# Two cached decode attentions on one core: A's keys and values by fours of heads, ahead of B's pairs

## The chip, the core and the metric

The kernel runs on one core of a Trainium2 chip. The metric is device time in microseconds, as the median of the runs; the kernel before took 249.97 us (three runs, 249.94 to 250.91). A profile is one further execution, taken with the hardware profiler.

## What is computed

Two independent attention blocks, A and B, decode one token each. Each has 32 query heads, 16 key/value heads of 128 elements and a cache of 8,192 keys; A uses only the last 2,048 of its keys, B uses all. Everything is bf16, and the two results are joined.

```python
    def _A_ref(x, k_cache, v_cache, wq, wo):
        B, Sq, D = x.shape
        Hq, Dh = 32, 128
        Hkv, Sk = k_cache.shape[1], k_cache.shape[2]
        W = min(4096, max(256, Sk // 4))
        rep = Hq // Hkv
        q = (lambda x, *d: x.transpose(*d))((x @ wq).reshape(B, Sq, Hq, Dh), 0, 2, 1, 3)
        k = jnp.repeat(k_cache[:, :, Sk - W:, :], rep, axis=1)
        v = jnp.repeat(v_cache[:, :, Sk - W:, :], rep, axis=1)
        scores = jnp.einsum("bhqd,bhkd->bhqk", q, k) * (Dh ** -0.5)
        p = _softmax(scores, axis=-1)
        o = jnp.einsum("bhqk,bhkd->bhqd", p, v)
        return (lambda x, *d: x.transpose(*d))(o, 0, 2, 1, 3).reshape(B, Sq, Hq * Dh) @ wo
...
    return jnp.concatenate([a, b], axis=-1)
```

B's function is the same without the slices of k and v.

The inputs that are read are A's K and V (16.8 MB), B's K and V (67.1 MB), two wq and two wo (18.9 MB together): 102.8 MB.

## The kernel before

The program is a list of operations per engine, in a hand-written order. `Prog.op` adds one to an engine with the names of those it depends on, `Prog.load` a DMA, and `emit` turns names into semaphore waits (L78). Each engine works its list strictly in order. All large loads are issued by SP (L208, L211, L219) into one SBUF ring of 144 KB a partition; `place` hands out the ring in order, and a load that overlaps an older one waits for that one's last reader. Because SP is in order too, a load that waits holds back the loads behind it.

The loads, in order: wq of A and of B (each 4 MB and a 0.5 MB tail), then for each of the eight pairs of key/value heads K of B (4 MB), K of A (1 MB), V of B, V of A; then wo of A in one piece and wo of B in six. A pair of B lies with 32 KB rows, head h on partitions 64h to 64h + 63. A pair of A has two rows of 4 KB on each partition, one for each head.

First the queries: x is brought onto the partitions (L263 to L280: `xd`, `xT`, `xr`), then `qmm` (L295) multiplies by wq in 16 groups of five matmuls, `qe` evicts, `qT` transposes on DVE, and `z0`, `z1` (L312, L318) copy the queries into `za` and `zb`, zero tiles that POOL has filled before (L236, L237). With the query columns at the right place of a zero tile, the scores of all slabs of a pair add up in one PSUM bank of 128x512: row 2s + r is slab s, query r.

Then for each pair p, in the order in which each engine has it:

- ten slabs of 2,048 elements, eight of B and two of A: DVE transposes K (`T`, L335) into one of three buffers `ktb`, and PE makes four matmuls of 128x512 (`S`, L345) from it;
- the maximum: `max` on DVE (L354), `mT` on PE (L356) to bring it into one row, `mrB`, `mrA`, `mxB`, `mxA` on DVE (L361 to L372) per head, `bc` on PE (L376) back to the partitions, `nb` on DVE (L378);
- `exp` on ACT (L380), with the row sums;
- `PT`: DVE transposes the weights, in two halves (L384);
- `V`: for each slab of B four matmuls of 128x512 in four column groups (L393), for each of A eight of 128x256 (L400);
- `xo0` on ACT (L407) and `xo1` on DVE (L409) evict, and `OB`, `OA` (L414, L421) fold the four groups with f32 matmuls into one column per head.

So on DVE the transposes of pair p + 1 stand behind `PT` and `xo1` of pair p, and on PE its scores stand behind `V`, `OB` and `OA` of pair p. At the end come `lsel`, `L`, `rl`, `on`, `oq`, `pm`, `oP` (the sums, the division and a regrouping, L430 to L446), the 128 output matmuls `F` (L457), a copy and the store.

Of the kernel before, what the change touches and what calls it, by code (L numbers as in the profile page):

```python
# [21 lines left out]
NB = 2 * SK // 128 * DH // SLAB  # L22
NI = NB + 2
W0 = 2 * (NB - 1)
ZW = 128 + W0
RING = 72 * 1024
# [80 lines left out]
def bass_concat_heads__sliding_block_cached__gqa_block_cached__decode_kernel(nc, A_x, A_k_cache, A_v_cache, A_wq, A_wo,  # L107
# [5 lines left out]

    ring = nc.alloc_sbuf_tensor("ring", [128, RING], BF16)
# [12 lines left out]
    za = nc.alloc_sbuf_tensor("za", [128, NP, 2, 4, 128], BF16)  # L127
    mx = nc.alloc_sbuf_tensor("mx", [128, 2], F32)
    mr = nc.alloc_sbuf_tensor("mr", [128, 8], F32)
    mexp = nc.alloc_sbuf_tensor("mexp", [128, 128], F32)  # L130
    nb = nc.alloc_sbuf_tensor("nb", [128, 2], F32)
# [4 lines left out]
    cls = nc.alloc_sbuf_tensor("cls", [128, 8], F32)  # L136
    selb = nc.alloc_sbuf_tensor("selb", [128, 16], F32)
    sela = nc.alloc_sbuf_tensor("sela", [128, 4], F32)
    par = nc.alloc_sbuf_tensor("par", [128, 2], F32)
    lsel = nc.alloc_sbuf_tensor("lsel", [128, NP, 8], F32)  # L140
    rl = nc.alloc_sbuf_tensor("rl", [128, NP * 8], F32)
# [60 lines left out]
    kv_at = {}  # L202
    for p in range(NP):
        for kind, c in (("K", ks), ("V", vs)):
            use = "T%d.%d" if kind == "K" else "V%d.%d"
            src = c[1][0, 2 * p:2 * p + 2, :, :].rearrange("h (q t) d -> (h q) (t d)", q=64)
            kv_at[kind, p, 0] = place(NB * SLAB, [use % (p, NB - 1)],
                                      lambda e, t, src=src: e.dma_start(t, src), "%sB%d" % (kind, p))  # L208
            src = c[0][0, 2 * p:2 * p + 2, SK - W_A:SK, :].rearrange("h (q t) d -> q h (t d)", q=128)
            kv_at[kind, p, 1] = place(2 * SLAB, [use % (p, NI - 1)],  # L210
                                      lambda e, t, src=src: e.dma_start(t.rearrange("q (h n) -> q h n", h=2), src),  # L211
                                      "%sA%d" % (kind, p))
# [10 lines left out]
    def slab(kind, p, s):  # L223
        t = kv_at[kind, p, s // NB]
        s %= NB
        return t[:, s * SLAB:(s + 1) * SLAB]
# [9 lines left out]
    op("pool", lambda e: e.memset(zb[:], 0.0), name="zb0")  # L236
    op("pool", lambda e: e.memset(za[:], 0.0), name="za0")  # L237
    op("pool", lambda e: e.memset(mexp[:], 0.0), name="mexp0")
    op("pool", lambda e: e.memset(onesf[:], 1.0), name="ones")
    op("pool", lambda e: e.memset(pts[:], 0.0), name="pts0")  # L240
# [3 lines left out]
    for b in range(2):  # L244
        op("dve", lambda e, b=b: e.memset(vb[b][:, :], 0.0), name="vb0.%d" % b)
# [3 lines left out]
    for h in range(2):  # L249
        op("dve", lambda e, h=h: e.tensor_reduce(  # L250
            cls[:, 2 * h:2 * h + 2], view(identf, 128, 64 * h, [[1, 2], [32, 2], [2, NB]]), AX.XY, ALU.add),
            deps=["identf"], name="clsB%d" % h)
    op("dve", lambda e: e.tensor_reduce(cls[:, 4:8], view(identf, 128, 2 * NB, [[1, 4], [32, 4]]), AX.X, ALU.add),
       deps=["identf"], name="clsA")
    op("dve", lambda e: e.tensor_reduce(selb[:], view(identf, 128, 0, [[1, 16], [32, 4]]), AX.X, ALU.add),
       deps=["identf"], name="selb")
    op("dve", lambda e: e.tensor_reduce(sela[:], view(identf, 128, 0, [[4, 2], [1, 2], [32, 4], [2, 2]]), AX.XY, ALU.add),
       deps=["identf"], name="sela")
# [3 lines left out]
    for P in range(2):  # L262
# [14 lines left out]
        for c in range(2):  # L277
            op("dve", lambda e, P=P, c=c: e.tensor_scalar(  # L278
                xrep[:, P, 4 + c, :], banks[2 * P + 1][:, 0:128], par[:, c:c + 1], None, ALU.mult),
                deps=["xT%d.4" % P, "par%d" % c], name="xr%d.%d" % (P, 1 + c))  # L280
    XR = ["xr%d.%d" % (P, c) for P in range(2) for c in range(3)]

    KT = NKT * SLAB
    for P in range(2):
        for n in range(8):
# [17 lines left out]
            else:  # L303
# [4 lines left out]
                deps=["qe%d" % u] + (["z0.%d" % i for i in range(8)] if P else []), name="qT%d" % u)  # L308
        srcs = [[512, NP], [64, 2], [1, 2], [128, 2]]
        for b in range(4):  # L310
# [5 lines left out]
            else:  # L316
                for h in range(2):
                    op("dve", lambda e, b=b, h=h: e.tensor_copy(  # L318
                        view(za, NP * 1024, h * 512 + 32 * b + 2 * (NB + h),
                             [[1024, NP], [256, 2], [128, 2], [1, 2]], 32, 32 * b),  # L320
                        view(ktb, KT, h * 256, srcs, 32, 32 * b)),
                        deps=["qT%d" % u for u in range(8)] + ["za0"], name="z0.%d" % (2 * b + h))
    Z = ["z0.%d" % i for i in range(8)] + ["z1.%d" % i for i in range(4)]


    def unit(kind, p, s):
        return "%s%s%d" % (kind, "BA"[s // NB], p)

    for p in range(NP):
        for s in range(NI):  # L330
            k = p * NI + s
            kt = ktb[:, (k % NKT) * SLAB:(k % NKT + 1) * SLAB]
            deps = [unit("K", p, s)]
            deps += ["S%d" % (k - NKT)] if k >= NKT else Z
            op("dve", lambda e, p=p, s=s, kt=kt: e.transpose(kt.bitcast(I32), slab("K", p, s).bitcast(I32)),  # L335
               deps=deps, name="T%d.%d" % (p, s))

# [12 lines left out]
            if s == 0:  # L350
                deps += ["exp%d" % (p - 2), "max%d" % (p - 2)] if p >= 2 else Z + ["qe%d" % u for u in range(16)]
# [153 lines left out]
```

## Time and profile before

Times in us. An execution has a span, from its first instruction to its last, and some time around it; the profiled one took 250.0 for a span of 248.2.

| what | value |
|---|---|
| median of the runs | 249.97 |
| the profiled execution; its span | 250.0; 248.2 |
| mean granted clock of PE | 0.82 |
| busy: PE, DVE, ACT, POOL | 181.7, 153.1, 18.1, 13.4 |
| DMA: packets, MB, GB/s over the span | 8,262, 102.92, 415 |
| packets under 8 KB | 5,564 |
| the chain that ended last: DMA, DVE, PE | 32%, 31%, 30% |
| K transposes L335 | 80 of 1.213, 92.4 |
| scores L345, from B and from A | 256 matmuls, 73.6; 64, 16.7 |
| V matmuls L393 (B) and L400 (A) | 256, 28.2; 128, 7.8 |
| folds L414 and L421 | 64 records each, 10.8 and 9.9 |
| output matmuls L457 | 128, 10.9 |

An engine's busy time says how much work it has, the chain says which work the end waited for, and the line of a group ends with the idle time ahead of it and what released it. PE's clock is granted at full or half rate, so the same matmul has two lengths: five of L295 take 2.14 us at 18.10 us, when PE has just begun, and 1.08 from 22.4 us on. Where a group's mean lies between, it mixes the two.

### The profile page before, as it was taken

Reading aid. Unit: us, or ns where it says so; the run is one execution under the profiler, and the core shown is the slowest. Engines: PE = TensorE matmul, PEld = TensorE weight load, DVE = VectorE, ACT = ScalarE, POOL = GpSimd, SP = SyncE. Lnnn points to the kernel's source line nnn. Section 1 sums busy time; section 2 is a strip of 40 time slices with the busy share of each in tenths; the row PEclk is TensorE's granted clock in tenths of the full one; section 3 lists DMA queues with packets and bytes.
Section 4 is the critical chain, followed back from the end, with each engine's and each line's share of the span. In section 5 each row is a group of like instructions: output and inputs, shape, how many; then the busy total and the mean of one; then the engine's idle time right before and its main releaser. Section 6 shows DMA issues by size and latency. Waiting matters only on the chain.

```text
span 248.2 us, 2581 instructions
## 1 busy us (share of the span) xinstructions
PE 181.7 (73%) x1085; PEld 80.7 (33%) x1085; DVE 153.1 (62%) x228; ACT 18.1 (7%) x36; POOL 13.4 (5%) x15
## 2 busy tenths in 40 slices
PE   0039994957995799379746984998489757975795
PEld 0013441313631342143224321732153124322552
DVE  8963779952885298439734873487349725972300
ACT  2001220010001000100010001000100010001000
POOL 8920000000000000000000000000000000000000
PEclk9999999795589599877987597569677957895769
DMA  7999999999999999999999999999999999999992
GB/s 264 418 490 433 422 422 416 417 428 418 427 414 434 419 458 419 436 432 431 421 429 414 434 422 428 420 422 419 433 420 433 428 433 422 436 403 457 395 406 111
DMA packets 8262, 102.92 MB, mean 415 GB/s; under 512 B 694, under 2 KB 956, under 8 KB 5564
## 3 DMA queue, kind: packets, MB, share of 16 engines
q1 hardware_dynamic: 8248, 102.77, 97.9%
q8 instruction: 8, 0.13, 0.2%
q14 instruction: 2, 0.02, 0.0%
q10 hardware_dynamic: 4, 0.00, 0.0%
HBM read 102.76 MB, written 0.00 MB: 414 GB/s over the span
## 4 chain that ended last, share of the span: by engine, by line
DMA 32%; DVE 31%; PE 30%; issue 3%; ACT 2%; SPq 0%; POOL 0%; POOLq 0%; DVEq 0%
DMA ring<-in_B_k_cache_dram 22%; DVE ktb L335 18%; DMA ring<-in_B_wo_dram 10%; PE sb L345 10%; PE vb L393 7%; DVE xdup L263 5%; PE sb L295 4%; PE qb L295 3%; DVE pts L384 3%; ACT psb L380 2%; PE ob L414 1%; DVE mx L354 1%; PE ob L421 1%; PE vb L400 1%; PE mb L356 1%
## 5 line engine op out<-in xcount | busy, mean ns | idle before, releaser
L335 DVE STREAM_TRANSPOSE ktb<-ring 128x1024 int32<-128x1024 int32 x80 | 92.4, 1213 | 11.3 <-DMA ring<-in_B_k_cache_dram 7.6
L345 PE MATMUL sb<-ktb,zb 128*128 128x512 bf16 x256 | 73.6, 443 | 11.0 <-DVE ktb L335 9.8
L345 PEld LDWEIGHTS sb<-ktb,zb 128*128 128x128 bf16 x256 | 25.6, 110 | 56.3 <-DVE ktb L335 24.2
L393 PE MATMUL vb<-ring,pts 128*16 128x512 bf16 x256 | 28.2, 619 | 21.1 <-DVE pts L384 21.1
L409 DVE COPY xo<-vb 128x512 f32<-128x512 f32 x8 | 5.5, 692 | 35.8 <-PE vb L400 35.8
L393 PEld LDWEIGHTS vb<-ring,pts 128*16 128x16 bf16 x256 | 8.5, 123 | 34.3 <-issue 34.2
L345 PE MATMUL sb<-ktb,za 128*128 128x512 bf16 x64 | 16.7, 381 | 1.3
L380 ACT ACTIVATE psb<-sb,nb 128x512 bf16<-128x512 f32 x8 | 5.5, 687 | 140.9 <-DVE nb L378 140.9
L384 DVE STREAM_TRANSPOSE pts<-psb 64x512 bf16<-64x512 bf16 x16 | 11.3, 706 | 7.0 <-ACT psb L380 6.8
L295 PE MATMUL sb<-ring,xrep 128*128 128x512 bf16 x40 | 11.2, 438 | 1.3 <-DVE xrep L278 1.3
L263 DVE COPY xdup<-xrow 1x128 bf16<-1x128 bf16 x2 | 11.3, 5660 | 0.0
L457 PE MATMUL qb<-ring,oP 128*1 128x288 bf16 x128 | 10.9, 346 | 0.5 <-DVE oP L446 0.4
L414 PEld LDWEIGHTS ob<-selb,xo 128*128 128x128 f32 x64 | 10.1, 242 | 3.4 <-ACT xo L407 3.4
L354 DVE TENSOR_REDUCE mx<-sb 128x1 f32<-128x512 f32 x8 | 5.5, 692 | 9.1 <-PE sb L345 9.1
L414 PE MATMUL ob<-selb,xo 128*128 128x4 f32 x64 | 10.8, 293 | 0.3 <-ACT xo L407 0.3
L272 PE MATMUL sb<-onesb,xrow 1*128 1x128 bf16 x4 | 0.6, 295 | 14.0 <-DVE xdup L263 14.0
L306 DVE STREAM_TRANSPOSE ktb<-qsb 128x256 int32<-128x256 int32 x16 | 7.0, 443 | 6.1 <-ACT qsb L301 5.8
L421 PE MATMUL ob<-sela,xo 128*128 128x2 f32 x64 | 9.9, 276 | 0.0
L421 PEld LDWEIGHTS ob<-sela,xo 128*128 128x128 f32 x64 | 9.5, 227 | 0.0
L295 PE MATMUL qb<-ring,xrep 128*128 128x512 bf16 x40 | 9.3, 379 | 0.0
L345 PEld LDWEIGHTS sb<-ktb,za 128*128 128x128 bf16 x64 | 4.9, 96 | 13.1 <-DVE ktb L335 9.2
L457 PEld LDWEIGHTS qb<-ring,oP 128*1 128x1 bf16 x128 | 6.1, 99 | 5.3 <-DMA ring<-in_B_wo_dram 1.2
(66 smaller groups left out, 83.0 us busy)
## 6 DMA issues: line engine op xcount, KB each, us to landing
ring<-in_B_k_cache_dram SPq DMA_DIRECT2D x8, 4096.0 KB, 27.0
ring<-in_B_v_cache_dram SPq DMA_DIRECT2D x8, 4096.0 KB, 26.8
ring<-in_A_k_cache_dram SPq DMA_DIRECT2D x8, 1024.0 KB, 28.9
ring<-in_A_v_cache_dram SPq DMA_DIRECT2D x8, 1024.0 KB, 27.2
ring<-in_A_wo_dram SPq DMA_DIRECT2D x1, 4608.0 KB, 28.2
ring<-in_A_wq_dram SPq DMA_DIRECT2D x1, 4096.0 KB, 12.2
ring<-in_B_wq_dram SPq DMA_DIRECT2D x1, 4096.0 KB, 22.3
ring<-in_B_wo_dram SPq DMA_DIRECT2D x1, 2304.0 KB, 33.4
```

The costliest lines, as they stand in the source:

```text
L263: op("dve", lambda e, P=P: e.tensor_copy(view(xdup, 256, 128 * P, [[2, 64], [1, 2]], parts=1), view(xrow, 2 * DM, P * DM + 512, [[1, 64], ...
L295: ins = e.matmul(bank[:, :], lhsT=lhsT, rhs=o, start=(k == 0), stop=(k == 4))
L306: op("dve", lambda e, n=n: e.transpose(ktb[:, n * 512:(n + 1) * 512].bitcast(I32), qsb[:, n % 2, :].bitcast(I32)), deps=["qe%d" % u] + ([" ...
L335: op("dve", lambda e, p=p, s=s, kt=kt: e.transpose(kt.bitcast(I32), slab("K", p, s).bitcast(I32)), deps=deps, name="T%d.%d" % (p, s))
L345: ins = e.matmul(sb[p % 2][:, :], lhsT=lhsT, rhs=view(ktb, KT, (k % NKT) * SLAB + 64 * c + v, [[128, 16], [2, 32]]), start=(s == 0 and c = ...
L354: op("dve", lambda e, p=p: e.tensor_reduce(mx[:, 0:1], sb[p % 2][:, :], AX.X, ALU.max), deps=["S%d" % (p * NI + NI - 1)] + (["mT%d" % (p - ...
L380: op("act", lambda e, p=p: e.activation(psb[:, :], sb[p % 2][:, :], ACT.Exp, bias=nb[:, p % 2:p % 2 + 1], scale=SCALE, accum_out=rsall[:, ...
L384: op("dve", lambda e, h=h: e.transpose(view(pts, 1024, 2 * h, [[4, 16], [64, 16], [1, 2]], 64, 64 * h), psb[64 * h:64 * h + 64, :]), deps= ...
L393: ins = e.matmul(vb[0][32 * j:32 * j + 16, :], lhsT=view(pts, 1024, 64 * s + 16 * j, [[1, 16]]), rhs=src[:, 512 * j:512 * j + 512], start= ...
L414: ins = e.matmul(ob[:, 8 * p:8 * p + 4], lhsT=xo[:, 0, 128 * t:128 * t + 128], rhs=selb[:, 4 * t:4 * t + 4], start=(t == 0), stop=(t == 3))
L421: ins = e.matmul(ob[:, 8 * p + 4 + 2 * h:8 * p + 6 + 2 * h], lhsT=xo[:, 1, 256 * h + 128 * t:256 * h + 128 * t + 128], rhs=sela[:, 2 * t:2 ...
L457: ins = e.matmul(fb[r:r + 1, 0:288], lhsT=oP[:, 1 - P, k0 + k:k0 + k + 1], rhs=wo_at[P, c][:, k * DM + 288 * n:k * DM + 288 * n + 288], st ...
```

## The change

- A's K and V are loaded before B's, in four units of four heads: row 4g + h of a load holds the 64 keys that start at 64g of head h, 16 KB, so that 8 loads of 2 MB take the place of 16 of 1 MB.
- Each unit has its own scores (four slabs in a bank of `qb`), maximum, exp, transpose `PA`, V matmuls, eviction `xoA` on ACT and fold `OA`. A partition holds one head, so a row of scores also has columns for keys of heads that are not its own; a matmul `mask` with -1e30 there starts the bank, and exp makes them 0.
- B's pairs have eight slabs in place of ten, and lose everything of A. `xo1` is gone from DVE; `xo` stays on ACT.
- The fills of `za`, `zb` and `pts` move from POOL to DVE, behind the preparation of x, and so do the small reductions for selectors; one of the two PSUM fills is gone. `za` shrinks from 8,192 to 2,432 elements a partition.
- The output columns lie by A and B, so that the product before `F` is plain.

The diff, cut:

```diff
 SLAB = 2048
-NB = 2 * SK // 128 * DH // SLAB
-NI = NB + 2
+ROW = 2 * SK // 128 * DH
+NB = ROW // SLAB
+NQ = G // 4
+TA = 4 * W_A // 128
+NA = TA * DH // SLAB
 W0 = 2 * (NB - 1)
 ZW = 128 + W0
+ZA = 128 + 24
+BIG = 1e30
 RING = 72 * 1024
 NSEM = 24
 NKT = 3
...
+    for u in range(NQ):
+        for kind, c in (("K", ks[0]), ("V", vs[0])):
+            src = bass.AP(tensor=c.tensor, offset=c.offset + (4 * u * SK + SK - W_A) * DH,
+                          ap=[[TA * DH, 32], [SK * DH, 4], [1, TA * DH]])
+            kv_at[kind, "A", u] = place(TA * DH, [("TA%d.%d" if kind == "K" else "VA%d.%d") % (u, NA - 1)],
+                                        lambda e, t, src=src: e.dma_start(t, src), "%sA%d" % (kind, u))
     for p in range(NP):
-        for kind, c in (("K", ks), ("V", vs)):
-            use = "T%d.%d" if kind == "K" else "V%d.%d"
-            src = c[1][0, 2 * p:2 * p + 2, :, :].rearrange("h (q t) d -> (h q) (t d)", q=64)
-            kv_at[kind, p, 0] = place(NB * SLAB, [use % (p, NB - 1)],
+        for kind, c in (("K", ks[1]), ("V", vs[1])):
+            src = c[0, 2 * p:2 * p + 2, :, :].rearrange("h (q t) d -> (h q) (t d)", q=64)
+            kv_at[kind, "B", p] = place(ROW, [("T%d.%d" if kind == "K" else "V%d.%d") % (p, NB - 1)],
                                       lambda e, t, src=src: e.dma_start(t, src), "%sB%d" % (kind, p))
-            src = c[0][0, 2 * p:2 * p + 2, SK - W_A:SK, :].rearrange("h (q t) d -> q h (t d)", q=128)
-            kv_at[kind, p, 1] = place(2 * SLAB, [use % (p, NI - 1)],
-                                      lambda e, t, src=src: e.dma_start(t.rearrange("q (h n) -> q h n", h=2), src),
-                                      "%sA%d" % (kind, p))
...
-    op("pool", lambda e: e.memset(zb[:], 0.0), name="zb0")
-    op("pool", lambda e: e.memset(za[:], 0.0), name="za0")
     op("pool", lambda e: e.memset(mexp[:], 0.0), name="mexp0")
     op("pool", lambda e: e.memset(onesf[:], 1.0), name="ones")
-    op("pool", lambda e: e.memset(pts[:], 0.0), name="pts0")
...
+
+    op("dve", lambda e: e.memset(za[:], 0.0), name="za0")
+    op("dve", lambda e: e.memset(zb[:], 0.0), name="zb0")
+    op("dve", lambda e: e.memset(pts[:], 0.0), name="pts0")
+    op("dve", lambda e: e.memset(vb[0][:, :], 0.0), name="vb0.0")
...
+    op("dve", lambda e: e.tensor_copy(mkr[:], view(ident, 128, 0, [[0, 128], [1, 4]], 4)),
+       deps=["ident"], name="mkr")
+    op("dve", lambda e: e.tensor_scalar(mkl[:], view(ident, 128, 0, [[0, 16], [1, 4], [0, 2]], 4), -1.0, BIG,
+                                        ALU.add, ALU.mult), deps=["ident"], name="mkl")
...
+                op("dve", lambda e, b=b: e.tensor_copy(
+                    view(za, NQ * 4 * ZA, ZA - 128 + 32 * b, [[4 * ZA, NQ], [2 * ZA, 2], [ZA, 2], [1, 8]], 32, 32 * b),
+                    view(ktb, KT, 0, [[1024, NQ], [64, 2], [1, 2], [128, 8]], 32, 32 * b)),
+                    deps=["qT%d" % u for u in range(8)] + ["za0"], name="z0.%d" % b)
+    Z = ["%s.%d" % (z, b) for z in ("z0", "z1") for b in range(4)]
+    QE = ["qe%d" % u for u in range(16)]
...
+    def scores(k, kind, src, name, lhsT, bank, start, stop, deps):
+        kt = ktb[:, (k % NKT) * SLAB:(k % NKT + 1) * SLAB]
+        op("dve", lambda e: e.transpose(kt.bitcast(I32), src.bitcast(I32)),
+           deps=[kind] + (["S%d" % (k - NKT)] if k >= NKT else Z), name=name)
+
+        def mm(e):
+            for c in range(2):
+                for v in range(2):
+                    ins = e.matmul(bank[:, :], lhsT=lhsT(2 * c + v),
+                                   rhs=view(ktb, KT, (k % NKT) * SLAB + 64 * c + v, [[128, 16], [2, 32]]),
+                                   start=(start and c == 0 and v == 0), stop=(stop and c == 1 and v == 1))
+            return ins
+        op("pe", mm, deps=[name] + deps, name="S%d" % k)
...
+    for u in range(NQ):
+        bank = qb[u % 2]
+        op("pe", lambda e, bank=bank: e.matmul(bank[:, :], lhsT=mkl[:].rearrange("p a h r -> p (a h r)"),
+                                               rhs=mkr[:].rearrange("p q h -> p (q h)"), start=True, stop=False),
+           deps=["expA%d" % (u - 2), "maxA%d" % (u - 2)] if u >= 2 else ["mkl", "mkr"] + QE, name="mask%d" % u)
+        for s in range(NA):
+            scores(u * NA + s, "KA%d" % u, slab("K", "A", u, s), "TA%d.%d" % (u, s),
+                   lambda ce, u=u, s=s: za[:, u, ce, ZA - 128 - 8 * s:ZA - 8 * s], bank, False, s == NA - 1, [])
+        op("dve", lambda e, bank=bank: e.tensor_reduce(mx[:, 4:5], bank[:, :], AX.X, ALU.max),
+           deps=["S%d" % (u * NA + NA - 1)] + (["mTA%d" % (u - 1)] if u else []), name="maxA%d" % u)
+        op("pe", lambda e: e.matmul(mb[0:1, 0:128], lhsT=mx[:, 4:5], rhs=identf[:, :], start=True, stop=True),
+           deps=["maxA%d" % u, "identf"] + (["mrA%d" % (u - 1), "nbA%d" % (u - 1)] if u else []), name="mTA%d" % u)
+        op("dve", lambda e: e.tensor_reduce(mr[0:1, 8:16], view(mb, 512, 0, [[1, 8], [8, 16]], parts=1), AX.X, ALU.max),
+           deps=["mTA%d" % u] + (["mxA%d" % (u - 1)] if u else []), name="mrA%d" % u)
+        op("dve", lambda e: e.tensor_scalar(
+            mexpa[:].rearrange("p (a m) -> p a m", m=8), view(mr, 32, 8, [[0, 16], [1, 8]], parts=1), -SCALE, None,
+            ALU.mult), deps=["mrA%d" % u] + (["bcA%d" % (u - 1)] if u else []), name="mxA%d" % u)
+        op("pe", lambda e: e.matmul(mb[:, 128:129], lhsT=mexpa[0:1, :], rhs=onesf[0:1, 0:1], start=True, stop=True),
+           deps=["mxA%d" % u, "ones"], name="bcA%d" % u)
+        op("dve", lambda e, u=u: e.tensor_copy(nb[:, 2 + u % 2:3 + u % 2], mb[:, 128:129]),
+           deps=["bcA%d" % u] + (["expA%d" % (u - 2)] if u >= 2 else []), name="nbA%d" % u)
+        op("act", lambda e, u=u, bank=bank: e.activation(psb[:, :], bank[:, :], ACT.Exp, bias=nb[:, 2 + u % 2:3 + u % 2],
+                                                         scale=SCALE, accum_out=rsa[:, u:u + 1]),
+           deps=["nbA%d" % u, "warm1"] + (["PA%d" % (u - 1)] if u else []), name="expA%d" % u)
+        op("dve", lambda e: e.transpose(view(pta, NA * 128, 0, [[8, 16], [128, NA], [1, 8]]), psb[:, :]),
+           deps=["expA%d" % u] + (["VA%d.%d" % (u - 1, NA - 1)] if u else []), name="PA%d" % u)
+        for s in range(NA):
+            def mm(e, u=u, s=s):
+                src = slab("V", "A", u, s)
+                for j in range(4):
+                    ins = e.matmul(vb[1][32 * j:32 * j + 32, :],
+                                   lhsT=pta[:, s, 4 * j:4 * j + 4, :].rearrange("p t k -> p (t k)"),
+                                   rhs=src[:, 512 * j:512 * j + 512], start=(s == 0), stop=(s == NA - 1))
+                return ins
+            op("pe", mm, deps=["VA%d" % u, "PA%d" % u] + (["xoA%d" % (u - 1)] if u else []), name="VA%d.%d" % (u, s))
+        op("act", lambda e: e.activation(xo[:, 1, :], vb[1][:, :], ACT.Copy),
+           deps=["VA%d.%d" % (u, NA - 1)] + (["OA%d" % (u - 1)] if u else []), name="xoA%d" % u)
+
+        def fold_a(e, u=u):
+            for t in range(4):
+                ins = e.matmul(ob[:, 8 * u:8 * u + 8], lhsT=xo[:, 1, 128 * t:128 * t + 128],
+                               rhs=sel[:, 8 * t:8 * t + 8], start=(t == 0), stop=(t == 3))
+            return ins
+        op("pe", fold_a, deps=["xoA%d" % u, "sel"], name="OA%d" % u)
+
 
     for p in range(NP):
-        for s in range(NI):
...
+        for s in range(NB):
+            scores(NQ * NA + p * NB + s, "KB%d" % p, slab("K", "B", p, s), "T%d.%d" % (p, s),
+                   lambda ce, p=p, s=s: zb[:, p, ce, W0 - 2 * s:W0 - 2 * s + 128], sb[p % 2], s == 0, s == NB - 1,
+                   (["exp%d" % (p - 2), "max%d" % (p - 2)] if p >= 2 else QE) if s == 0 else [])
+        op("dve", lambda e, p=p: e.tensor_reduce(mx[:, 5:6], sb[p % 2][:, :], AX.X, ALU.max),
+           deps=["S%d" % (NQ * NA + p * NB + NB - 1)] + (["mT%d" % (p - 1)] if p else []), name="max%d" % p)
...
         op("act", lambda e: e.activation(xo[:, 0, :], vb[0][:, :], ACT.Copy),
-           deps=["V%d.%d" % (p, NB - 1)] + (["OB%d" % (p - 1)] if p else []), name="xo0.%d" % p)
-        op("dve", lambda e: e.tensor_copy(xo[:, 1, :], vb[1][:, :]),
-           deps=["V%d.%d" % (p, NI - 1)] + (["OA%d" % (p - 1)] if p else []), name="xo1.%d" % p)
+           deps=["V%d.%d" % (p, NB - 1)] + (["OB%d" % (p - 1)] if p else []), name="xo%d" % p)
...
+                ins = e.matmul(ob[:, HQ + 4 * p:HQ + 4 * p + 4], lhsT=xo[:, 0, 128 * t:128 * t + 128],
+                               rhs=sel[:, 4 * t:4 * t + 4], start=(t == 0), stop=(t == 3))
...
-        op("pe", fold_b, deps=["xo0.%d" % p, "selb"], name="OB%d" % p)
-        op("pe", fold_a, deps=["xo1.%d" % p, "sela"], name="OA%d" % p)
+        op("pe", fold_b, deps=["xo%d" % p, "sel"], name="OB%d" % p)
...
+        lsel[:, 0, :].rearrange("p (u m) -> p u m", m=8), rsa[:, :].unsqueeze(2).to_broadcast([128, NQ, 8]),
+        view(clsa, 8, 0, [[0, NQ], [1, 8]]), ALU.mult), deps=["expA%d" % (NQ - 1), "clsa"], name="lselA")
...
-                        ins = e.matmul(fb[r:r + 1, 0:288], lhsT=oP[:, 1 - P, k0 + k:k0 + k + 1],
+                        ins = e.matmul(fb[r:r + 1, 0:288], lhsT=oP[:, P, k0 + k:k0 + k + 1],
```

## The prediction

> **What bounds the kernel now.** I read the page's slices and queues first, to see whether the DMA engines ever rest; then the chain of waits at the end, for what the last microseconds hang on; then the timeline of one pair, for the slack of the compute; last the granted clock.
>
> ```profile
> DMA  7999999999999999999999999999999999999992
> ...
> q1 hardware_dynamic: 8248, 102.77, 97.9%
> ...
> L335 DVE STREAM_TRANSPOSE ktb<-ring 128x1024 int32<-128x1024 int32 x80 | 92.4, 1213 | 11.3 <-DMA ring<-in_B_k_cache_dram 7.6
> ```
>
> The DMA engines are full from the second slice to the last but one. But the K transposes on DVE waited only 7.6 us in all for K data: compute follows close behind. The end of the chain of waits (start, length, what):
>
> ```profile
> 181.21 27.33 DMA ring<-in_B_k_cache_dram
> ...
> 208.57 1.26 DVE ktb L335
> ...
> 219.43 25.99 DMA ring<-in_B_wo_dram
> 245.47 0.30 PE qb L457 x2
> ```
>
> The last pair's K lands at 208.5, wo's last piece at 245.4. Compute needs 208.57 to 234.7 for that pair and 11.0 us for the output matmuls (L457 from 234.72 to 245.76, idle 0.5): it ends with the DMA. Two clocks are tied. Now a pair for which nothing waits for data (p = 1 to 2):
>
> ```profile
> 81.92 3.59 PE L393 MATMUL vb<-ring,pts 128*16 128x512 bf16 x32 [2.63 <-DVE pts L384]
> 85.56 0.60 ACT L407 ACTIVATE xo<-vb 128x512 f32<-128x512 f32 x1 [5.26 <-PE vb L393]
> 86.30 1.36 PE L414 MATMUL ob<-selb,xo 128*128 128x4 f32 x8
> 86.41 0.69 DVE L409 COPY xo<-vb 128x512 f32<-128x512 f32 x1 [4.64 <-PE vb L400]
> 87.14 11.38 DVE L335 STREAM_TRANSPOSE ktb<-ring 128x1024 int32<-128x1024 int32 x10
> 88.44 8.93 PE L345 MATMUL sb<-ktb,zb 128*128 128x512 bf16 x32
> ...
> 99.65 0.69 DVE L354 TENSOR_REDUCE mx<-sb 128x1 f32<-128x512 f32 x1 [1.14 <-PE sb L345]
> ...
> 102.90 1.44 DVE L384 STREAM_TRANSPOSE pts<-psb 64x512 bf16<-64x512 bf16 x2 [0.85 <-ACT psb L380]
> ```
>
> A pair is serial: V on PE, xo, ten transposes with the scores behind them, then the softmax from max (99.65) to PT's end (104.34), 4.7 us, with PE almost idle. PT end to PT end is 81.77 to 104.34, 22.6 us (24.7 for p = 0 to 1, where PE was slow). The DMA's beat is 24.6 a pair. Compute has 0 to 2 us of slack a pair, so **the length of this serial chain is what I price**, next to the DMA.
>
> **DMA.** Same bytes. In the trace's packet records 4,096 B takes 162.7 ns on its engine, 32,768 B 1,222.7. The line through both has 11.3 ns a packet and 0.0370 a byte: 617 ns for 16,384 B. A's K and V: before 4,096 x 162.7 / 16 = 41.7 us, after 1,024 x 617 / 16 = 39.5: 2.2 less (bounds: 0, if 16 KB rows run at the 4 KB rate, to 2.5, at the 32 KB rate). From the first packet at 1.8, wq takes 22.2, A 39.5, each 4 MB of B 128 x 1,222.7 / 16 = 9.8. Such sums come 1.2 early (wq 24.0, landed 25.2), so KB0 lands at 74.5, KB7 at 211, wo at 243.2.
>
> A's 4 KB rows already step 2 MiB from head to head, and those figures show no price for it. [...]
>
> **Start.** xd0, a 1x128 copy, is booked from 2.78 to 13.9 while POOL fills zb and za; its twin took 0.20:
>
> ```profile
> 2.78 11.12 DVE L263 COPY xdup<-xrow 1x128 bf16<-1x128 bf16 x1
> ...
> 5.71 6.92 POOL L237 MEMSET za<- 128x8192 bf16 x1
> ```
>
> With the fills on DVE behind xr, xr ends near 7.5. Fills and small operations (8,000 elements at 0.47 to 0.95 ns, 0.95 being the 512-element memset's 0.485 us, and 2 us) end by 17 at worst, beside qmm0. That waits for wq0.1, issued 1.19 and 13.0 to landing: 14.2 in place of 18.1. It needs 10.8 (18.1 to 28.9), to 25.0; wq1.1 lands at 25.2; qmm1 takes 40 x 0.216 = 8.6, to 33.9; the transposes begin 2.2 later, as before (37.5 to 39.7): 36.1, a gain of 3.6. If POOL had not been what held xd0, this gain is 0.
>
> **The clock decides the rest.** The columns are the stretch, its length, L393's PE and PEld time, the granted clock, DMA:
>
> ```profile
> 56.23:59.64 3.41, 2.42 (x24) 0.91 (x28) 0.50 0.96 408
> 59.64:63.06 3.42, 1.17 (x12) 0.15 (x4) 0.50 1.19 493
> 104.02:107.43 3.41, 2.94 (x29) 1.06 (x32) 0.50 1.05 452
> 107.43:110.84 3.41, 0.39 (x8) 0.00 (x0) 1.00 1.05 426
> ```
>
> The clock changes only on a grid of 3.41 us. Each idle softmax drops it to 0.5. A stretch with 2.9 us of V brings it back, one with 2.4 does not, nor did 59.64 to 63.06, which PE filled, though mostly with A's narrow V and the f32 fold. I count a stretch as warming from 2.65 us of wide bf16 matmul on.
>
> **A's four units, new, ahead of all of B.** From PA's end (0): V, four groups of four matmuls at 0.43 as in L393, to 1.9; xo on ACT to 2.5; the f32 fold 1.05 (full clock) to 1.87 (half); the mask matmul 0.2 to 0.4; four slabs of four matmuls at 0.216 or 0.43. Then max 0.74, mT 0.42, mr and mx of 128 elements 0.5, bc 0.42, nb 0.2, exp 0.83, PA 0.75 (512 elements, as one of L384; 1.44 at most): 3.85, in which no later transpose runs, because DVE has them behind it. Period 11.3 full, 15.2 half. V is 1.7 long and cannot warm PE; scores from 4.5 on do, 2.65 later at the earliest, at 7.1 to 10.6 by the grid: 13.5 to 15.2. I take 14.3. Unit 0: transposes from 36.1, scores done 43.0, PA0 at 46.9. PA3: 46.9 + 42.9 = **89.8**; KB0 has waited 15 us.
>
> **B's pairs.** Removed: two slabs (2.3 of DVE), A's V matmuls, OA, mrA, mxA, and xo1, which held DVE until V was done: now three transposes run beside V. From PT's end: V 0.14 to 3.73, xo to 4.45, OB to 5.5 (6.3 half), first slab to 6.6, transposes 4 to 8 at 1.15 to 12.45, last scores 1.1, softmax 4.5: 18.1. If V did not warm PE (half of the grid's positions leave less than 2.65 of its 3.59 in one stretch), slabs run at 1.7 until 9 to 12: 19.7 to 20.5. Half and half: 19.2. Eight: 153.6, PT7 ends at **243.4**.
>
> The DMA's beat of 19.6 a pair leaves the lag as it is. The ring nearly holds it: VB1 is issued after VA3.3, 91.7, the queue is busy to 94; KB2 after T0.7, 103, busy to 104. wo waits for V6.7, 228, and its first piece lands near 241, ahead of use. SP issues 24 K and V loads in place of 32, hidden behind a full queue; if it were dry, eight of 0.4 would be 3 us.
>
> [...]
>
> **Tail.** PT7's end to the span's end was 226.2 to 248.2, 22.0. OA's 0.75 ahead of L goes, and some waiting for wo: 21.0 (at most 22.0).
>
> **Sum.** 36.1 + 10.8 + 42.9 + 153.6 + 21.0 = 264.4 of span, against 248.2. The profiled run took 250.0, 1.8 more than its span (the median is 249.97): 264.4 + 1.8 = **266**. In one view: the softmax and PE's refill behind it are paid twelve times in place of eight, 54 us ahead of B, and B gives back 3 to 4.5 a pair, the start 3.6.
>
> **Rivals.** (1) *Level.* PE stays warm: 45.9 + 33.9 + 7 x 18.1 = 206.5, before KB7 lands at 211. Then the pair takes its 17.65 (208.57 to 226.22) less 2.5, to 226.4, and 21.0: 247.4 + 1.8 = **249**. For it: six of eight pairs had the clock back before the scores. Against: A's V and OA stood behind V there. It decides once compute gains 1.8 us a pair on this sum.
> (2) *Faster.* As (1), and wo's matmuls at full clock (F1's 64 took 4.1, F0's 6.9): the DMA's end rules, 243.2 + 2.8 + 1.8 = **248**. Against: PE idles ahead of F0 each time.
> (3) *Cold.* Half clock throughout: 46.9 + 45.6 + 8 x 20.8 + 21 + 1.8 = **282**. For it: p = 0 and 4 were cold over most scores. Against: six were not.
> That the change does not do what it says is excluded by its address pattern; its packets can be counted.
>
> **Chances.** Forecast 0.76, rival 1 0.10, rival 2 0.06, rival 3 0.08. The forecast's own range, from 18.3 to 20 a pair and 13.5 to 15.2 a unit, is 257 to 275. The 80% range is 252 (units and pairs a quarter of the way from full clock to my values) to 274. A change of 0.5%, 1.25 us, is about what a measurement of this kernel tells from none: faster 0.07, within 0.11, slower 0.82.
>
> **What would show it.** Right: packets fall by 3,072 and 8 x 16 to about 5,060; xd0 near 0.2 us and the first K transpose near 36; PA's 13 to 15 apart; B's first transpose near 90 and no wait for K data after it; pairs 18 to 20.5 apart; a DMA row below 9 late in the span. Wrong: B's transposes waiting for K again by p = 4 (rival 1); units near 11.3; A's packets well over 650 ns.

## The result, and the profile after

The changed kernel took 257.60 us (median of four runs, 256.47 to 259.27) against 249.95 for the kernel before (four runs, 249.91 to 250.91): 1.0302 times as long, 95% interval 1.0227 to 1.0377, or 7.65 us slower. The forecast was 266 us, 16 slower, with 252 to 274 as its 80% range. Direction and mechanism held; the increase was forecast twice as large as it came.

The profiled execution took 258.65, with a span of 256.8 and a mean clock of 0.827 (before 250.0, 248.2 and 0.820). From its page, the lines that were read of the one before (slices, the chain by engine, the K transposes):

```profile
PEclk9999986659595958989799569799569799579779
DMA  8999999999999999999999999999999999899930
...
PE 54%; DVE 30%; ACT 7%; DMA 5%; issue 3%; SPq 0%; DVEq 0%
...
L343 DVE STREAM_TRANSPOSE ktb<-ring 128x1024 int32<-128x1024 int32 x80 | 93.3, 1215 | 38.0 <-PE sb L349 28.0
```

Read the second row first. Before, the DMA engines were full to the last slice but one; now the row ends in 3 and 0: the loads end near 246 us (the share is 0.48 in the stretch from 244.64 to 248.05, and 0.00 in the next), and some 10 us of compute follow. In the chain that ended last, DMA falls from 32% to 5%, nearly all of it wq at the start, and PE rises from 30% to 54%. The K transposes waited 11.3 us before, most of it for K; now 38.0, most of it for PE's scores to free a `ktb` buffer. No wait for K data is left in B. The bound has gone from DMA-with-compute-close-behind to compute alone.

Now one pair of B twice, from the chain of waits (start, length, engine and line, instructions). First p = 1 to 2, PT's end to PT's end 17.8 us; then p = 2 to 3, 20.1:

```profile
125.31 3.53 PE vb L437 x32
...
129.51 1.05 PE ob L447 x8
...
131.50 5.76 DVE ktb L343 x5
...
143.09 3.62 PE vb L437 x31
...
147.38 1.87 PE ob L447 x8
149.25 3.41 PE sb L349 x8
...
152.68 4.64 DVE ktb L343 x4
```

V is as long in both. After it the fold takes 1.05 in the one and 1.87 in the other, and where five transposes on DVE set the pace in the first, eight score matmuls at 0.43 each come into the chain in the second: PE is at half clock. What decides between them is in the stretches of 3.41 us at whose ends alone the granted clock changes in this profile, its grid (the columns are the stretch, its length, the time of V's matmuls L437 on PE and PEld, the granted clock, the DMA share, GB/s):

```profile
125.17:128.58 3.41, 3.27 (x32) 1.06 (x32) 0.50 1.02 442
128.58:131.99 3.41, 0.23 (x4) 0.00 (x0) 1.00 1.07 461
142.24:145.65 3.41, 2.56 (x28) 0.94 (x32) 0.50 1.00 432
145.65:149.06 3.41, 1.03 (x12) 0.11 (x4) 0.50 1.07 456
```

In the first pair V fills 3.27 us of one stretch, and the next stretch has the full clock. In the second V starts 0.85 us into its stretch, 2.56 us of it fall there, and the next stretch stays at half. Over the eight pairs the clock came back after 2.88 to 3.27 us and did not after 2.38 to 2.56. A pair whose V brings the clock back is called warm below, the other cold.

### The profile page after: what moved, and what is told of

The parts are those of the page before. It is cut to its first block, busy times and chain, and to the rows that moved or that the text cites. A ratio compares the mean times of both kernels' runs of the same rounds, so it can differ in the third digit from the quotient of the medians.

```text
span 256.8 us, 2423 instructions
## 1 busy us (share of the span) xinstructions
PE 181.0 (70%) x1008; PEld 78.0 (30%) x1009; DVE 148.2 (58%) x224; ACT 23.6 (9%) x48; POOL 1.8 (1%) x12
## 2 busy tenths in 40 slices
DMA packets 5062, 102.91 MB, mean 401 GB/s; under 512 B 566, under 2 KB 828, under 8 KB 1340
## 4 chain that ended last, share of the span: by engine, by line
PE 54%; DVE 30%; ACT 7%; DMA 5%; issue 3%; SPq 0%; DVEq 0%
DVE ktb L343 16%; PE vb L437 11%; PE sb L349 10%; PE qb L349 9%; DMA ring<-in_A_wq_dram 5%; DVE pts L429 4%; PE sb L311 4%; PE ob L447 4%; PE qb L482 3%; PE qb L311 3%; PE ob L396 3%; ACT psb L425 2%; DVE mx L407 2%; PE vb L386 2%; ACT xo L442 2%
## 5 line engine op out<-in xcount | busy, mean ns | idle before, releaser
L349 PE MATMUL sb<-ktb,zb 128*128 128x512 bf16 x256 | 67.4, 411 | 1.6
L437 PE MATMUL vb<-ring,pts 128*16 128x512 bf16 x256 | 27.5, 607 | 21.1 <-DVE pts L429 21.1
L349 PE MATMUL qb<-ktb,za 128*128 128x512 bf16 x64 | 22.5, 524 | 2.8 <-DVE ktb L343 2.8
L437 PEld LDWEIGHTS vb<-ring,pts 128*16 128x16 bf16 x256 | 8.6, 123 | 34.2 <-issue 34.1
L429 DVE STREAM_TRANSPOSE pts<-psb 64x512 bf16<-64x512 bf16 x16 | 11.3, 707 | 7.0 <-ACT psb L425 6.8
L447 PE MATMUL ob<-sel,xo 128*128 128x4 f32 x64 | 10.9, 293 | 5.6 <-ACT xo L442 5.6
L447 PEld LDWEIGHTS ob<-sel,xo 128*128 128x128 f32 x64 | 10.2, 242 | 12.1 <-ACT xo L442 12.1
L349 PEld LDWEIGHTS qb<-ktb,za 128*128 128x128 bf16 x64 | 7.6, 124 | 17.3 <-issue 11.9
L386 PE MATMUL vb<-ring,pta 128*32 128x512 bf16 x64 | 5.0, 442 | 7.6 <-DVE pta L380 7.6
L396 PE MATMUL ob<-sel,xo 128*128 128x8 f32 x32 | 7.5, 364 | 2.8 <-ACT xo L391 2.8
L396 PEld LDWEIGHTS ob<-sel,xo 128*128 128x128 f32 x32 | 7.1, 328 | 5.2 <-ACT xo L391 5.2
L442 ACT ACTIVATE xo<-vb 128x512 f32<-128x512 f32 x8 | 4.8, 597 | 40.9 <-PE vb L437 40.9
L364 DVE TENSOR_REDUCE mx<-qb 128x1 f32<-128x512 f32 x4 | 2.8, 690 | 9.8 <-PE qb L349 9.8
L311 PEld LDWEIGHTS sb<-ring,xrep 128*128 128x128 bf16 x40 | 4.2, 108 | 11.5 <-issue 8.1
## 6 DMA issues: line engine op xcount, KB each, us to landing
ring<-in_B_v_cache_dram SPq DMA_DIRECT2D x8, 4096.0 KB, 20.7
ring<-in_A_wo_dram SPq DMA_DIRECT2D x1, 4608.0 KB, 14.7
ring<-in_B_wo_dram SPq DMA_DIRECT2D x1, 2304.0 KB, 19.9
```

The lines of the kernel that those rows point to most:

```text
L311: ins = e.matmul(bank[:, :], lhsT=lhsT, rhs=o, start=(k == 0), stop=(k == 4))
L349: ins = e.matmul(bank[:, :], lhsT=lhsT(2 * c + v), rhs=view(ktb, KT, (k % NKT) * SLAB + 64 * c + v, [[128, 16], [2, 32]]), start=(start an ...
L386: ins = e.matmul(vb[1][32 * j:32 * j + 32, :], lhsT=pta[:, s, 4 * j:4 * j + 4, :].rearrange("p t k -> p (t k)"), rhs=src[:, 512 * j:512 * ...
L396: ins = e.matmul(ob[:, 8 * u:8 * u + 8], lhsT=xo[:, 1, 128 * t:128 * t + 128], rhs=sel[:, 8 * t:8 * t + 8], start=(t == 0), stop=(t == 3))
L429: op("dve", lambda e, h=h: e.transpose(view(pts, 1024, 2 * h, [[4, 16], [64, 16], [1, 2]], 64, 64 * h), psb[64 * h:64 * h + 64, :]), deps= ...
L437: ins = e.matmul(vb[0][32 * j:32 * j + 16, :], lhsT=view(pts, 1024, 64 * s + 16 * j, [[1, 16]]), rhs=src[:, 512 * j:512 * j + 512], start= ...
```

## The experiments

Each kernel is an edit of the changed kernel, unless it says "before". The names T, S, max, PA, V and so on are those of the operations; a number behind PA or PT is that of the unit or pair, and its time is that of its end. In the runs that follow the kernel before had medians of 249.99 to 250.09.

**1 and 2. Is it DMA or compute?** Only the first half of each row of B's V is loaded, and slabs 4 to 7 use slabs 0 to 3 again: the number of instructions is unchanged, 16.8 MB of traffic are gone. It was done to both kernels; the edit of the changed one:

```diff
-                                      lambda e, t, src=src: e.dma_start(t, src), "%sB%d" % (kind, p))
+                                      lambda e, t, src=src, kind=kind: e.dma_start(t[:, 0:ROW // 2], src[:, 0:ROW // 2]) if kind == "V"
+                                      else e.dma_start(t, src), "%sB%d" % (kind, p))
...
-                src = slab("V", "B", p, s)
+                src = slab("V", "B", p, s % (NB // 2))
```

> The changed kernel, but of B's V only the first half of each row is loaded, and the V matmuls of slabs 4 to 7 read slabs 0 to 3 again: every instruction of the engines stays, and the DMA has 16.8 MB less, 39 us by its own packet times. Theory (the serial chain of transposes, scores, softmax and V sets the time, the DMA is beside it): 255 to 259, as with all of V (257.6). Rival (the DMA queue or the ring sets it, with A's units ahead): under 245.

> The kernel before with the same cut: half of B's V rows not loaded, the V matmuls unchanged in number. Theory: its DMA and its chain of compute were tied, with 7.6 us of waits for K data: without these 238 to 244, which is what its compute alone needs; the changed kernel's compute alone is 256, so the change made the compute some 15 us longer. Rival (compute is about as long in both, and the change lost on the DMA side): both kernels with the cut within 4 us of each other.

The changed kernel took 256.73 (ratio to the kernel before 1.0262, 1.0223 to 1.0302), as without the edit. The kernel before took 240.28 (237.44 to 241.76 in four runs; ratio 0.956, 0.9491 to 0.963). The K transposes of the changed kernel with the edit, then of the one before with it (their lines moved by one):

```profile
L344 DVE STREAM_TRANSPOSE ktb<-ring 128x1024 int32<-128x1024 int32 x80 | 93.3, 1215 | 37.5 <-PE sb L350 28.0
```

```profile
L336 DVE STREAM_TRANSPOSE ktb<-ring 128x1024 int32<-128x1024 int32 x80 | 92.0, 1213 | 2.1 <-PE sb L346 1.8
```

The changed kernel is bound by compute alone: the same waits for PE remain, 28.0 us, and the time with them. The kernel before has a compute of about 240 under a DMA of 250. So the change adds some 16.5 us of compute (256.73 less 240.28), of which 10 fill the wait that was there, and the rest shows. That is the answer to "where did the time come from". The profile of the changed kernel and that of the kernel before with the edit split it: the first K transpose comes 3.0 earlier (36.86 against 39.84), A's units take 53.0 (36.86 to 89.83), the first pair 0.6 more, B's other seven pairs 130.6 in place of 158.5, 27.9 less, and the tail, from the last PT's end, 1.5 less: 21.2 between these two executions, whose spans are 256.8 and 235.6 (the second was the fastest of its four runs).

**3. Is it the place ahead of B?** A's unit u, loads and operations, is put behind B's pairs 2u and 2u + 1.

```diff
+    ORDER = [x for u in range(NQ) for x in (("B", 2 * u), ("B", 2 * u + 1), ("A", u))]
+    for side, i in ORDER:
...
+    for side, i in ORDER:
+        if side == "A":
+            unit_a(i, MT, EX)
+            MT, EX = ["mrA%d" % i, "nbA%d" % i], ["PA%d" % i]
+        else:
+            pair_b(i, MT, EX)
+            MT, EX = ["mrB0.%d" % i, "mrB1.%d" % i, "nb%d" % i], ["PT0.%d" % i, "PT1.%d" % i]
```

> The changed kernel with A's units not ahead of B but one behind every two pairs, loads and operations alike; the number of units, pairs and softmax chains is the same. Theory (what costs is that the chain is gone through twelve times): 254 to 260. Rival (what costs is the place ahead of B, where B's first data lies idle for 15 us while the DMA runs ahead): 251 or less.

257.72 (1.0306, 1.0249 to 1.0363): the same. The order of A and B is not the cause, nor is B's late start as such: the twelve serial softmaxes cost the same in both orders.

**4. How much of it is A's softmax chain?** A's maximum is left out, from `maxA` to `nbA`; the exp takes a bias of 0.

```diff
-        op("dve", lambda e, bank=bank: e.tensor_reduce(mx[:, 4:5], bank[:, :], AX.X, ALU.max),
...
-        op("act", lambda e, u=u, bank=bank: e.activation(psb[:, :], bank[:, :], ACT.Exp, bias=nb[:, 2 + u % 2:3 + u % 2],
+        op("act", lambda e, u=u, bank=bank: e.activation(psb[:, :], bank[:, :], ACT.Exp, bias=nb[:, 2:3],
```

> The changed kernel without A's maximum (max, mT, mr, mx, bc and nb are left out of A's four units, exp has a bias of 0). These six are 0.74 + 0.42 + 0.5 + 0.42 + 0.2 = 2.3 us of each unit's chain. Theory: 9 us less, or somewhat less where DMA data is waited for again: 248 to 251. Rival (these latencies are hidden by the DMA): within 2 us of 257.6.

249.11 (0.9953, 0.9923 to 0.9984), 8.5 us less than the changed kernel. Units came 8.4, 10.0 and 10.0 apart in place of 14.4, 13.6 and 13.6, PA3 ended at 74.39, and B's transposes waited for K again:

```profile
L344 DVE STREAM_TRANSPOSE ktb<-ring 128x1024 int32<-128x1024 int32 x80 | 93.2, 1216 | 40.6 <-DMA ring<-in_B_k_cache_dram 29.6
```

A unit lost 3.6 to 6.0 us, more than the 2.3 of the six operations; the clock was granted at 0.83 to 1.00 over these three units, where it was 0.70 to 0.75. Taking 15 us out of A gave back 8.5 and no more: the rest became waits for K, 29.6 us in all. When B waits for its K, the loads and the work behind the last K set the time, here near 249.

**5. How much is PE's clock?** Matmuls whose result nobody reads are put where PE idles in each softmax: four ahead of mT, four ahead of bc, eight (A) or twelve (B) ahead of V.

```diff
+            op("pe", lambda e: e.matmul(bank[:, 0:320], lhsT=ident[:, :], rhs=view(zb, NP * 4 * ZW, 0, [[1, 320]]),
+                                        start=True, stop=True), deps=deps, name=names[-1])
...
+            idle(4, "mT%s%d" % (c, i), bank, deps)
+            idle(4, "bc%s%d" % (c, i), bank, deps)
+            idle(o, "V%s%d.0" % (c, i), bank, deps)
```

> The changed kernel with matmuls that do nothing useful (128x320, into a bank that is free at the time) in PE's idle stretches of every softmax: 4 ahead of mT, 4 ahead of bc, 8 or 12 ahead of V. Theory (a unit is 11.3 and a pair 17.6 with PE's clock full, and 13.6 to 14.4 and 20.0 after a drop): the granted clock near 1.0, units near 11.5, all pairs near 17.6 or waiting for K data, and 248 to 251. Rival (the clock is not what the units' 13.6 and the pairs' 20.0 come from, or the fill delays the chain as much as it gains): 255 or more.

249.46 (0.9971, 0.9953 to 0.9989), at a mean clock of 0.945.

```profile
PEclk9999997999979999999999799599799799999799
...
L343 DVE STREAM_TRANSPOSE ktb<-ring 128x1024 int32<-128x1024 int32 x80 | 92.6, 1213 | 30.5 <-DMA ring<-in_B_k_cache_dram 23.6
```

More work on PE, 8 us less time. Units came 10.8, 10.8 and 12.4 apart, the pairs 15.3, 16.2 and 16.7 until K data set the pace, then 19 to 20. PT7 ended at 226.77. This is the prediction's rival 1 made true: it put PT7 at 226.4 and the time at 249. The first three pairs were shorter than the 17.6 expected, since V ran at full clock too (379 ns a matmul in place of 607).

**6. The same fillers on the kernel before**, to see what is left between the two kernels when both have more of the clock (0.945 and 0.882 in the profiles).

> The kernel before with matmuls that do nothing useful in PE's idle stretches, 4 ahead of mT, 4 ahead of bc and 12 ahead of V of each pair. The changed kernel with the like took 249.46. Theory (both are then set by the DMA, and A's 16 KB rows are worth about 2 us of it at most): 249 to 251, between 0 and 2 us above the changed kernel with them. Rival (the change has no part in that time; the clock alone is): 249.0 or less.

251.16 (1.003, 1.0004 to 1.0057): no gain there, since DMA sets its end (its chain ends with 26.8 us of wo's loads), and 1.7 us above the changed kernel with fillers. PT7 ends no later here (226.31 against 226.77); the difference lies behind it, where the output matmuls wait for wo. A's 16 KB rows would explain it: wo's first packet starts at 218.8 in the changed kernel with fillers and at 220.5 here. The rows were not changed alone, so this is a fit and not shown.

**7 and 8. Can the softmax be hidden behind the next item's work?** The next item's first transpose goes ahead of this one's max on DVE, its second ahead of PA or PT, its first two slabs' scores ahead of V on PE and the third ahead of the fold. In all twelve items; and likewise in the kernel before.

```diff
+        move("dve", [T[0]], ("maxA%d" if c == "A" else "max%d") % i)
+        move("dve", [T[1]], ("PA%d" if c == "A" else "PT0.%d") % i)
+        move("pe", (["mask%d" % j] if d == "A" else []) + S[0:2], ("VA%d.0" if c == "A" else "V%d.0") % i)
+        move("pe", [S[2]], ("OA%d" if c == "A" else "OB%d") % i)
```

> The changed kernel with operations moved in the engines' lists, nothing added: the next unit's or pair's first transpose ahead of max, its second ahead of PA or PT, its first two slabs of scores (and A's mask) ahead of V, and the third ahead of the fold. The softmax then runs beside the next scores. Theory: a unit falls to 8 to 10 us and a pair under 17, the DMA's beat of 19.6 sets the time, B's transposes wait for K data again, and the time is 247 to 250, with A's longer rows worth 2 us at most. Rival (DVE in order behind K data, or the moved scores, delay the chain): 253 or more.

> The kernel before with the same moves (third transpose ahead of xo1). Theory: it was tied between DMA and compute; now the DMA alone sets it: 248 to 250, and the two pipelined kernels differ by the 2 us of A's packets or less. Rival (the moves gain a compute-bound kernel as much as the one after): 245 or less.

253.89 (1.0142, 1.0105 to 1.018) and 255.13 (1.0198, 1.0173 to 1.0223). Both miss their expectation; on the kernel before the moves even lose 5 us. The timeline of the changed kernel with the moves, at the last K of B, shows why (start, length, engine, line, operation; in brackets the idle time ahead and what ended it):

```profile
211.84 1.25 DVE L343 STREAM_TRANSPOSE ktb<-ring 128x1024 int32<-128x1024 int32 x1 [5.37 <-DMA ring<-in_B_k_cache_dram]
213.01 0.65 DVE L407 TENSOR_REDUCE mx<-sb 128x1 f32<-128x512 f32 x1
213.72 0.59 PE L409 MATMUL mb<-identf,mx 128*1 128x128 f32 x2 [6.15 <-DVE mx L407]
```

DVE waits 5.37 us for the last pair's K, and behind that wait stands the maximum of the pair before, whose data were long there; PE has idled for 6.15. Each pair's softmax now begins only when the next pair's K has landed, so the last two pairs are worked off after the last K: PT6 at 218.13, PT7 at 232.06, against 226.8 in experiment 5. In the kernel before with the moves, DVE waited 44.1 us for B's K in all, where it had waited 7.6, and PT7 ended at 233.52, where it had ended at 226.22. A move that hides a chain where the data are ahead exposes it where they are not.

**9. So only where the data are there: the same moves among A's four units alone.**

```diff
+    for u in range(NQ - 1):
...
+        move("dve", [T[0]], "maxA%d" % u)
+        move("dve", [T[1]], "PA%d" % u)
+        move("pe", ["mask%d" % (u + 1)] + S[0:2], "VA%d.0" % u)
+        move("pe", [S[2]], "OA%d" % u)
```

> The changed kernel with the moves among A's four units alone: the next unit's first two transposes ahead of max and PA, its mask and first two slabs of scores ahead of V, the third ahead of the fold; B as in the change. In the kernel that was pipelined throughout, the time was 253.9, and each pair's softmax stood behind the wait for the next pair's K data. Theory (that wait is what cost; without it, A's units at 8 to 10 us leave B a lag of some 3 to 6 us, and B's pairs of 18.5 against a beat of 19.6 work it off): 249 to 252. Rival (pipelining costs in another way): 253 or more.

248.69 (0.9944, 0.9925 to 0.9963), 8.9 us below the changed kernel and 1.3 below the one before. Units came 9.2, 9.8 and 9.3 apart, PA3 ended at 75.65, and B waits for K again:

```profile
L343 DVE STREAM_TRANSPOSE ktb<-ring 128x1024 int32<-128x1024 int32 x80 | 93.5, 1217 | 35.6 <-DMA ring<-in_B_k_cache_dram 16.2
```

**10 and 11. Is the earlier start worth its 3 us, and was POOL what held the copy?** First six fills of a tile that nobody reads were put on POOL behind `identf`, each waiting for the one before. Then the fills of zb, ktb, za and pts were put on POOL with no wait between them; those of zb, za and pts are gone from DVE.

```diff
-    op("dve", lambda e: e.memset(za[:], 0.0), name="za0")
-    op("dve", lambda e: e.memset(zb[:], 0.0), name="zb0")
-    op("dve", lambda e: e.memset(pts[:], 0.0), name="pts0")
...
+    op("pool", lambda e: e.memset(zb[:], 0.0), name="zb0")
+    op("pool", lambda e: e.memset(ktb[:], 0.0), name="ktb0")
+    op("pool", lambda e: e.memset(za[:], 0.0), name="za0")
+    op("pool", lambda e: e.memset(pts[:], 0.0), name="pts0")
```

> The changed kernel with six POOL fills of 128x2048 ahead of everything x needs from DVE, so that the preparation of x is held until about 14 us again, as before the change. Theory (the chain of compute carries every delay to the end, and the first transpose moves from 36.9 to about 39.7): 2 to 4 us more, 259 to 262. Rival (the DMA or the lag of B hides the start): within 1 us of 257.6.

> The changed kernel with the fills of zb, za and pts back on POOL ahead of mexp, with a fill of ktb (128x6144) among them, so that POOL is busy without a pause until about 14 us, as before the change. Theory (xd0 waits for POOL, and the chain carries every delay to the end): xd0 ends near 14, the first transpose moves from 36.9 to about 39.7, and the time is 1.5 to 4 us more than 257.6, 259 to 262. Rival (the start is not set by POOL): xd0 near 2.6 and 257.6 within 1 us.

The first one took 256.98 (1.0284, 1.0246 to 1.0321) and missed its aim: the copy was held 1.52 us only, for one fill, and the start was not late; it says nothing on what a late start costs. The second took 259.67 (1.0369, 1.033 to 1.0407). From the timelines, the copy `xdup` in the first kernel, then the copy and the first K transposes in the second:

```profile
2.24 1.52 DVE L264 COPY xdup<-xrow 1x128 bf16<-1x128 bf16 x1
```

```profile
2.24 12.01 DVE L265 COPY xdup<-xrow 1x128 bf16<-1x128 bf16 x1
...
40.24 4.62 DVE L344 STREAM_TRANSPOSE ktb<-ring 128x1024 int32<-128x1024 int32 x4
```

With the fills back on POOL the copy is again booked for 12 us, the first transpose is at 40.24 in place of 36.86, and from PA3 on every step is 3.4 later too: PA3 93.26, PT7 241.63, span 260.2 against 256.8, with the same pair lengths to 0.05 us. This is the longest of the four runs (258.75 to 262.09); by medians it is 2.1. So POOL's fills did hold the copy, and the late start is seen at the end. It is not simply carried there: PA0 is only 1.7 later (49.88 against 48.20), since PE was done sooner in unit 0 (its maximum waited 1.14 for the scores where it had waited 2.84; the unit is 9.6 long in place of 11.3), and the next two units, 15.3 and 14.5 long in place of 14.4 and 13.6, lose the rest again. The 3.4 us are almost one stretch of the clock's grid, so the pairs kept their place on it; another delay could change a pair's length as well.

**The runs side by side.** One profiled execution each; the median is that of all runs. Pairs are from PT's end to PT's end, the first from PA3 on.

| kernel | median | units | PA3 | pairs | PT7 | waited for B's K |
|---|---|---|---|---|---|---|
| changed | 257.60 | 14.4, 13.6, 13.6 | 89.83 | 17.8, 17.6, 17.8, 20.1, 17.6, 20.0, 17.6, 20.0 | 238.19 | 0 |
| no maximum in A | 249.11 | 8.4, 10.0, 10.0 | 74.39 | 16.1, 19.4, 19.7, 19.3, 19.3, 20.7, 20.7, 20.7 | 230.25 | 29.6 |
| fillers on PE | 249.46 | 10.8, 10.8, 12.4 | 80.93 | 15.3, 16.2, 16.7, 19.6, 20.4, 19.0, 19.4, 19.2 | 226.77 | 23.6 |
| moves in all | 253.89 | 8.5, 10.1, 14.7 | 81.10 | 20.1, 19.6, 19.4, 19.6, 19.4, 19.4, 19.4, 13.9 | 232.06 | 42.8 |
| moves in A alone | 248.69 | 9.2, 9.8, 9.3 | 75.65 | 19.0, 20.7, 17.9, 17.8, 17.5, 19.9, 19.2, 19.0 | 226.53 | 16.2 |

In the changed kernel A's units end near 90 and nothing waits; in the other four B waits for its K by the end, and the time is that of the DMA and of what each leaves to do after the last K.

## Why the prediction was wrong in size, and where it was right

**The start, right.** The held copy took 0.40, 10.7 us less, and its twin 0.21; the first K transpose was forecast at 36.1:

```profile
2.24 0.40 DVE L261 COPY xdup<-xrow 1x128 bf16<-1x128 bf16 x1
...
36.86 4.62 DVE L343 STREAM_TRANSPOSE ktb<-ring 128x1024 int32<-128x1024 int32 x4 [0.51 <-DVE zb L328]
```

The gain is 2.8 (39.70 to 36.86) where 3.6 was expected.

**DMA, right, and off the path.** Packets fell from 8,262 to 5,062 (forecast about 5,060), those of 16 KB took 618.5 ns (617), so A's loads take 39.6 us of DMA (1,024 x 618.5 / 16) where they took 41.7. The 2.1 us gained can show only where compute is out of the way: 1.7 lie between experiments 5 and 6.

**A's units, right.** PA0 at 48.2 (46.9), units of 14.4, 13.6 and 13.6 (14.3), PA3 at 89.83 (89.8): unit 0 was 1.3 late, the others 1.3 short in sum, so the exact hit at PA3 is luck. A unit of 13.6 is four stretches of the grid (13.65). "Paid twelve times in place of eight" is what experiments 3, 4, 5 and 9 confirm: not the place, but the serial chain and the half clock behind it.

**B's pairs: the step that failed.** It reads: "half of the grid's positions leave less than 2.65 of its 3.59 in one stretch ... Half and half: 19.2." The 2.65, an estimate from rows with 2.42 and 2.94, held for these pairs (back at 2.88, not at 2.56). The size of a warm pair was 17.6 to 17.8 (18.1), of a cold one 20.0 to 20.1 (19.7 to 20.5). But five of eight pairs were warm, not four: 148.4 in all where 153.6 was forecast, 18.5 a pair in place of 19.2. The positions are not drawn evenly from the grid. A warm pair of 17.6 us is 5.15 stretches of 3.413, so V starts 0.5 us later in its stretch than the time before; a cold one of 20.0 is 5.86, which sets it 0.5 earlier. A V late in its stretch makes a long pair, and the long pair sets the next V earlier again: from p = 2 on the starts go .85, .44, 1.01, .51, 1.03, .53 into the stretch. Of the 5.2 us missing, one warm pair more is some 2.4, the rest the 0.3 to 0.5 us by which each pair was shorter than its estimate.

Two more rows bear on the 2.65. In experiment 10's first kernel the clock came back after a stretch with 2.59 us of V, a little less than that. And in the kernel before it came back after 1.97 us of B's V with 1.08 of A's narrow V (L400) and 0.66 of the f32 fold (L414) behind it, and not after 1.17 with the same 1.08 and 1.47 of the fold, though PE was busy for all 3.42 us of that stretch. Read so, the narrow V counts, against the prediction's reading, and the fold does not, or not in full; these two stretches are all that is behind it. The changed kernel has no such narrow V, so the sum is untouched. First two stretches of experiment 10's first kernel, V alone, then two of the kernel before, B's V alone:

```profile
141.95:145.36 3.41, 2.59 (x28) 1.01 (x32) 0.50 1.03 442
145.36:148.78 3.42, 0.57 (x12) 0.07 (x4) 1.00 1.05 446
...
83.54:86.95 3.41, 1.97 (x20) 0.46 (x12) 0.50 1.10 450
86.95:90.36 3.41, 0.00 (x0) 0.00 (x0) 1.00 1.00 429
```

In all these rows the clock stands at 0.50 or at 1.00 for a whole stretch of 3.41 us; where V's wide matmuls were alone, it came back after 2.59 us of them and did not after 2.56.

**The tail, 2.4 too long.** 18.6 from PT7's end to the span's end, where 21.0 was taken from before. The output matmuls:

```profile
245.51 8.75 PE L482 MATMUL qb<-ring,oP 128*1 128x288 bf16 x128 [0.41 <-DVE oP L471]
```

They took 11.04 before, when two stretches, 233.72 to 240.55, had half clock over them; here only 244.64 to 248.05 has. Again the place on the grid, which the sum had carried over from the kernel before as if it were a duration.

Pairs and tail, 5.2 and 2.4, are the 7.6 us between the forecast span of 264.4 and 256.8. The four runs of the changed kernel, 256.5 twice, 258.7 and 259.3, lie over 2 us apart, and only the second longest was profiled, so why they differ stays open. It need not be a cold pair: the profile of experiment 1, with a span of 254.7 like the two shorter runs (254.6 and 254.8), has the same three cold pairs, and its PA3 is 2.0 earlier (87.84). Experiment 10's first kernel had two cold pairs, but a tail of 20.7 in place of 18.6, for a span of 255.7.

**The rivals.** Rival 1 (level, 249) did not come about, but with PE kept warm the time was 249.46. Its price was right because K's landing sets PT7; its pairs of 18.1 were 15.3 to 16.7 before they waited. Rival 2 (DMA end) came nearest in experiment 9, 248.69 against its 248, by another way: the units were pipelined, not warmed. Rival 3 (cold throughout, 282) had no support.

## What to carry to other kernels

Before splitting a serial step off to be done on its own, count how often its chain is paid, and compare the compute alone, measured with part of the traffic taken away, with the DMA's floor: here 16.5 us of compute were added to a kernel with 10 us of room. Put the next item's work ahead of a serial chain only where its data are certain to be there (A's units); where they arrive just in time (B's pairs), an in-order engine then holds this item's chain behind the next one's load, as DVE did for 5.37 us at the last K of experiment 7. When a clock moves on a grid, as PE's did here in steps of 3.41 us, a loop's period decides its phase: work out the sequence of starts from the period, rather than take each place on the grid as equally likely.

## What was not expected of the hardware

A one-partition copy on DVE of 0.20 us was held for 12.01 us by fills on POOL that follow each other without a wait, through several of them, and for 1.52 by fills of 1.85 with a semaphore wait between them. So here it did not get in between two fills that had no wait between them; what holds it there the traces do not show.

The zero fill of za on DVE, a bf16 tile of 2,432 elements a partition, stands in the timeline on 4-byte words, as 128x1216 uint32, and took 1.07 us, 0.44 ns an element, below the 0.47 to 0.95 by which it was bounded (0.47 was an estimate, half of the 0.95 of an f32 fill).

Keeping an engine busy with work that nobody needs shortened the changed kernel by 8 us (257.60 to 249.46), and did not shorten the one before (250.00 to 251.16).
